# Attention in steps of 128 queries instead of 64, the first two blocks in alternating halves, and a new order

## The chip, the cores and the metric

The kernel runs on one core of a Trainium2 chip. TensorE (PE) multiplies matrices into PSUM, VectorE (DVE), ScalarE (ACT) and GpSimd (POOL) work element by element, and SyncE (SP) issues the loads and stores, which 16 DMA engines carry. Everything is one launch. The metric is the time of one execution in microseconds; lower is better. The time before is 1117.62 us, the median of three runs (1113.61 to 1118.52).

## What is computed

Local attention with eight memory keys feeds a rational feed-forward layer, and that feeds a gated one:

```python
# q, k, v: 4 batches x 8 heads x 768 x 64; for each chunk of 32 queries
k_full = concat([mem_k, k[c_start-16 : c_end+8]])          # 64 keys
a = softmax(q_c @ k_full.T / 8);  attn = a @ v_full
x  = attn as 3072 tokens x 512
h  = x @ w_in                                              # 512 -> 2048
P  = a[0] + a[1]*h + a[2]*h**2 + a[3]*h**3
Q  = 1 + |b[0]|*|h| + |b[1]|*h**2
x2 = (P / (Q + 1e-6)) @ w_out                              # 2048 -> 512
out = ((x2 @ w1) * (x2 @ w2)) @ w3 @ w_out2                # 512 -> 1024 -> 1024 -> 512
```

## The kernel before

**Blocks and units.** The 3072 tokens are eight blocks of 384. The first layer (`ffn1`) goes through 128 *units*, 16 for each block; unit n takes one slice of 128 of the 2048 hidden columns. A unit is twelve matmuls into a PSUM tile `h` (`gemm1`), a chain of elementwise steps on ACT, DVE and POOL (the functions `rat_...`, `g_hi`, `g_lo`; the four tiles are `W`, `Q`, `A` and `h`), and twelve matmuls that add to four PSUM banks `acc` (`gemm2`). Each product is three matmuls, since every operand is kept as a high part and a low part. `SEQ` lists the units. Before the change block 0 does its first eight slices, then block 1 all sixteen, then block 0 its other eight; at each such change of block the four `acc` banks are put away (`spill`), and block 0's first half is read back (`half_back`) and added (`half_add`).

**Weights.** They come as 64-bit numbers, 512 KB for each slice of 128. `decode` turns a slice into its high and low part: ACT and DVE shift and join the bits (`scale`, `low`, `join`), ACT writes the high part, DVE or POOL the low part. The 16 slices of `w_in` go to `wA`, those of `w_out` to `wB`, and all 32 are decoded while the first two blocks run. `MODES` says for each slice which engines and which PSUM ring (`h` or `att`) it uses.

**Attention.** A step `u` takes 64 queries of all heads: loads (`load_qk`, `load_v`), scores on PE (`s_pe`), maximum, difference, exponential, sum, inverse and product (`s_max` to `s_norm`), transposes (`t_pe`), a copy by ACT and one by DVE into `aT` (`t_copy`), the product with v (`v_pe`), and the split of the result into the two parts of `xr`, which is the block's x (`v_parts`). Six steps make a block. `qk`, `v` and `e` have two buffers each. Chunk 0's keys stand together in the loaded tile; chunk 1's are the memory keys and the last 56, which DVE or POOL copy into a second tile `k` (`second_keys`, L291). The norm runs on POOL (L343). From block 1 on, the outputs of a step and the scores of the next are one piece of PE work in one PSUM bank (`vs_pe`), and the ring `att`, from which these pieces and the transposes take their bank, has one bank.

**After the first layer** the program makes the gate's products for blocks 0 and 1 (`ab`), the product of w3 and the last weights (`w3o`), and then blocks 2 to 7 in pairs (`pr`) with the last product (again `acc`, 512 wide).

**Order.** `order()` is a planner that runs when the program is built. Every piece of work is a `step` with a due time, an assumed cost for each engine that can do it, what it comes after, and what buffers it takes and frees. Due times are in units and come from tables (`R`, `DI`, `SI`, `TG`, `XT` and others). It decides the order in which instructions stand on each engine, and the engine itself where there is a choice; on the chip each engine then takes its instructions in that order and waits for what each one needs.

## Time and profile before

| what | value |
|---|---|
| median of three runs | 1117.62 us (1113.61 to 1118.52) |
| the profiled execution, and its span | 1116.94 us, 1115.2 us |
| PE, DVE, ACT, POOL busy | 1061.4, 763.4, 700.4, 511.3 us |
| data moved, mean rate | 104.03 MB, 93 GB/s |

The span runs from the first to the last instruction of the profiled execution; 1.74 us lie around it. Matmuls follow one another in a pipeline, so a PE that is busy all the time still goes faster or slower with what stands in its queue; its time is read from the starts of its matmuls. The stretches in the rows below are cut at events of this program: the first matmul into `h` (46.24 us), the first `h` of unit 8 (105.76), the end of the `h` of unit 39 (256.6), a point in the units of block 7 (612), the end of the `h` of the last unit (675.5), a point just after the first `w3o` (745), and one after the last `w3o` and the waits behind it (840).

### The profile page before, as it was taken

What the parts mean: (1) busy time and instruction counts of PE and PEld (TensorE: products, weight loads), DVE (VectorE), ACT (ScalarE), POOL (GpSimd) and SP (SyncE); (2) the same over time, 40 slices, a digit from 0 to 9 for tenths busy, and PEclk for the clock granted to TensorE, in tenths of its full rate; (3) what the DMA queues carried; (4) which work ended last, traced back from release to release, by engine and by line L of the source; (5) the groups of instructions that cost most, each with busy time, mean ns of one, the idle gap of its engine ahead of it and who ended that gap; (6) DMA issues with size and microseconds to landing.
All of it is one profiled execution on the core that took longest, in us unless ns stands there. A gap on an engine that the chain in (4) does not pass through costs nothing.

```text
span 1115.2 us, 20447 instructions
## 1 busy us (share of the span) xinstructions
PE 1061.4 (95%) x7632; PEld 989.4 (89%) x7632; DVE 763.4 (68%) x1495; ACT 700.4 (63%) x1363; POOL 511.3 (46%) x513
## 2 busy tenths in 40 slices
PE   5587899999999999999999998999999999999998
PEld 3486888989999999999999998998779999998997
DVE  5888989778687777677777887776564662563330
ACT  3686998768687787777877997744343252343322
POOL 1454665445454454444444566642223343335233
PEclk9998999999999999999999999999999999999999
DMA  8835331322121121111220324643433321312201
GB/s 220 231 96 171 115 109 52 110 71 63 44 71 43 52 82 44 56 57 44 79 84 35 114 76 133 208 134 131 134 131 114 114 85 50 112 39 78 74 20 57
DMA packets 42468, 104.03 MB, mean 93 GB/s; under 512 B 6208, under 2 KB 6336, under 8 KB 42368
## 3 DMA queue, kind: packets, MB, share of 16 engines
q1 hardware_dynamic: 42080, 102.65, 29.2%
q8 instruction: 60, 0.98, 0.4%
q14 instruction: 40, 0.33, 0.1%
q10 hardware_dynamic: 288, 0.07, 0.0%
HBM read 85.14 MB, written 17.56 MB: 92 GB/s over the span
## 4 chain that ended last, share of the span: by engine, by line
PE 72%; DVE 12%; ACT 8%; DMA 5%; issue 2%; SPq 1%; POOL 0%; DVEq 0%; POOLq 0%; ACTq 0%
PE acc L275 27%; PE h L275 18%; PE pr L275 14%; PE ab L275 5%; PE w3o L275 3%; DMA qk<-in_qkT_dram 3%; PE at L365 2%; PE at L312 2%; DVE w L248 2%; ACT A L399 1%; DVE A L416 1%; ACT Q L407 1%; ACT W L399 1%; DMA sr<-sd 1%; ACT Q L423 1%
## 5 line engine op out<-in xcount | busy, mean ns | idle before, releaser
L275 PE MATMUL h<-xr,wA 128*128 128x384 f32 x1536 | 296.4, 342 | 11.6 <-DVE A L437 8.6
L275 PE MATMUL acc<-gh,wB 128*128 128x384 f32 x1024 | 287.0, 343 | 1.5 <-POOL wB L259 1.2
L275 PEld LDWEIGHTS h<-xr,wA 128*128 128x128 f32 x1536 | 270.3, 190 | 16.8 <-DVE A L437 10.8
L411 POOL TENSOR_TENSOR W<-W,Q 128x384 f32<-128x384 f32 x128 | 130.8, 1022 | 168.3 <-ACT Q L407 116.9
L275 PEld LDWEIGHTS acc<-gh,wB 128*128 128x128 f32 x1024 | 188.0, 190 | 5.6 <-POOL wB L259 1.9
L275 PE MATMUL acc<-gl,wB 128*128 128x384 f32 x512 | 173.4, 339 | 1.9 <-POOL gl L446 1.9
L446 POOL TENSOR_TENSOR gl<-A,gh 128x384 fp32r<-128x384 f32 x128 | 132.0, 1032 | 51.2 <-ACT gh L441 41.4
L275 PE MATMUL pr<-wB,wA 128*128 128x384 f32 x624 | 114.4, 335 | 1.0 <-ACT W L932 0.9
L429 DVE SCALAR_TENSOR_TENSOR A<-A,cf,h 128x384 f32<-128x384 f32 x128 | 77.9, 608 | 51.6 <-ACT h L425 51.1
L275 PEld LDWEIGHTS pr<-wB,wA 128*128 128x128 f32 x624 | 108.9, 188 | 3.2 <-ACT W L932 1.2
L275 PEld LDWEIGHTS acc<-gl,wB 128*128 128x128 f32 x512 | 97.1, 190 | 3.3 <-POOL gl L446 3.3
L399 ACT ACTIVATE A<-h,cf 128x384 f32<-128x384 f32 x128 | 85.1, 665 | 22.7 <-PE h L275 21.9
L423 ACT ACTIVATE Q<-W,one 128x384 f32<-128x384 f32 x128 | 78.6, 614 | 28.4 <-POOL W L411 28.1
L407 ACT ACTIVATE Q<-W,cf 128x384 f32<-128x384 f32 x128 | 90.7, 709 | 3.8
L275 PE MATMUL acc<-wB,gh 128*128 128x512 f32 x294 | 92.2, 394 | 0.0
L416 DVE TENSOR_TENSOR A<-A,h 128x384 f32<-128x384 f32 x128 | 70.2, 548 | 30.1 <-ACT W L399 16.8
L441 ACT CAST gh<-A 128x384 fp32r<-128x384 f32 x128 | 64.8, 506 | 39.3 <-DVE A L437 39.0
L939 POOL TENSOR_TENSOR A<-A,Q 128x384 f32<-128x384 f32 x24 | 24.5, 1020 | 124.1 <-DVE A L939 124.1
L418 DVE SCALAR_TENSOR_TENSOR A<-A,cf,h 128x384 f32<-128x384 f32 x128 | 77.9, 609 | 2.9 <-ACT W L399 0.8
L433 DVE SCALAR_TENSOR_TENSOR h<-W,one,h 128x384 f32<-128x384 f32 x128 | 78.5, 614 | 0.1
L939 DVE TENSOR_TENSOR A<-pr,W 128x384 f32<-128x384 f32 x48 | 26.7, 556 | 69.5 <-PE pr L275 68.9
L437 DVE SCALAR_TENSOR_TENSOR A<-h,A 128x384 f32<-128x384 f32 x128 | 70.4, 550 | 1.3
(123 smaller groups left out, 1846.3 us busy)
## 6 DMA issues: line engine op xcount, KB each, us to landing
qk<-in_qkT_dram SPq DMA_DIRECT2D x96, 160.0 KB
w<-in_w_out_dram SPq DMA_DIRECT2D x24, 512.0 KB
sr<-sd SPq DMA_DIRECT2D x48, 256.0 KB
w<-in_w_in_dram SPq DMA_DIRECT2D x16, 512.0 KB
w<-in_w3T_dram SPq DMA_DIRECT2D x16, 512.0 KB
w<-in_w_dram SPq DMA_DIRECT2D x16, 512.0 KB
v<-in_vW_dram SPq DMA_DIRECT2D x48, 128.0 KB
out_dram<-oo SPq DMA_DIRECT2D x24, 256.0 KB
```

What stands on the lines that cost most here:

```text
L275: pe.matmul(out_, lhsT=wi(w, a), rhs=xi(x, c), start=first and i == 0, stop=last and i == 2, skip_group_check=more)
L399: act.activation(out=t, in_=hps[n][src], func=func, scale=scale, bias=bias)
L407: act.activation(out=t, in_=hps[n]["W"], func=AF.Identity, scale=cf[:, 5:6], bias=cf[:, 4:5])
L411: pool.tensor_tensor(out=W, in0=W, in1=Q, op=ALU.mult)
L416: dve.tensor_tensor(out=A, in0=A, in1=h, op=ALU.mult)
L418: dve.scalar_tensor_tensor(out=A, in0=A, scalar=cf[:, 1:2], in1=h, op0=ALU.add, op1=ALU.mult)
L423: act.activation(out=Q, in_=W, func=AF.Ln, bias=one)
L429: dve.scalar_tensor_tensor(out=A, in0=A, scalar=cf[:, 0:1], in1=r, op0=ALU.add, op1=ALU.mult)
L433: dve.scalar_tensor_tensor(out=r, in0=W, scalar=one, in1=r, op0=ALU.add, op1=ALU.mult)
L437: dve.scalar_tensor_tensor(out=A, in0=r, scalar=-2.0, in1=A, op0=ALU.add, op1=ALU.mult)
L441: act.copy(out=gh, in_=hps[n]["A"])
L446: eng.tensor_tensor(out=gl, in0=hps.pop(n)["A"], in1=gt[n].bitcast(F32), op=ALU.subtract)
```

## The change

Attention goes in steps of 128 queries (two windows of 64 side by side, `NS` = 2). `qk`, `v` and `e` have one buffer each instead of two. A copy of the memory keys is kept behind each window in the tile, loaded once a batch, so both chunks find their 64 keys in a row and the copies into `k` are gone. The norm may go to POOL or DVE; the planner puts all 24 on DVE. Scores and outputs are separate pieces of PE work. Blocks 0 and 1 alternate in halves: eight units of block 0, eight of block 1, then the second halves, so both put a half away and add it later. The constant 1 + 1e-6 of the rational function is an immediate instead of a tile `one`. The planner's costs, due times, `MODES` and the leads of attention are new. The matmuls are the same in number and shape.

```diff
+NS = 2
+UQ = NS * QB
+UPS = S // UQ
+NU = B * UPS
-UPB = N // QB
+UPB = N // UQ
-HF = NF1 // 2
-SEG = [(0, 0, HF), (1, 0, NF1), (0, HF, NF1)] + [(b, 0, NF1) for b in range(2, NB)]
+HF = 8
+SEG = [(0, 0, HF), (1, 0, HF), (0, HF, NF1), (1, HF, NF1)] + [(b, 0, NF1) for b in range(2, NB)]
...
-    q_t = atp.tile([P, 2, HG, QB + KW], F32, name="qk")
-    k_t = [atp.tile([P, HG, CK], F32, name=f"k{i}") for i in range(2)]
-    v_t = [atp.tile([P, H, D], F32, name=f"v{i}") for i in range(2)]
-    e_t = [atp.tile([P, 2 * NCH, CK], F32, name=f"e{i}") for i in range(2)]
+    q_t = [atp.tile([P, HG, NS, QB + KW + NMEM], F32, name=f"qk{i}") for i in range(QBUF)]   # QBUF = 1
+    v_t = [atp.tile([P, NS, H, D], F32, name=f"v{i}") for i in range(VBUF)]                  # VBUF = 1
+    e_t = [atp.tile([P, NG, CK], F32, name=f"e{i}") for i in range(EBUF)]                    # EBUF = 1
...
     def load_qk(u):
+        b, j = divmod(u, UPS)
+        t = q_t[u % QBUF]
         for g in range(2):
-            sp.dma_start(out=q_t[g * D:(g + 1) * D, u % 2], in_=qkT[b, j, :, g * HG:(g + 1) * HG])
-    def second_keys(u, mem, eng):
-        k = slice(0, NMEM) if mem else slice(W1, KW)
-        eng.tensor_copy(out=k_t[u % 2][:, :, :NMEM] if mem else k_t[u % 2][:, :, NMEM:],
-                         in_=q_t[:, u % 2, :, QB + k.start:QB + k.stop])
+            r, h = slice(g * D, (g + 1) * D), slice(g * HG, (g + 1) * HG)
+            for s in range(NS):
+                sp.dma_start(out=t[r, :, s, :QB + KW], in_=qkT[b, j * NS + s, :, h])
+            if j < QBUF:
+                for s in range(NS):
+                    sp.dma_start(out=t[r, :, s, QB + KW:], in_=qkT[b, 0, :, h, QB:QB + NMEM])
...
-    def s_norm(u):
-        e = e_t[u % 2]
-        pool.tensor_tensor(out=e, in0=e, in1=sums.pop(u).to_broadcast([P, 2 * NCH, CK]), op=ALU.mult)
+    def s_norm(u, eng):
+        e = e_t[u % EBUF]
+        eng.tensor_tensor(out=e, in0=e, in1=sums.pop(u).to_broadcast([P, NG, CK]), op=ALU.mult)
...
-    def vs_pe(u, tag, outputs, scores):
-        b = bank(tag, "at")
-        if outputs:
-            v_pe(u, b[:, :KC * QB])
-        if scores:
-            s_pe(u + 1, b[:, KC * QB:])
...
-            act.activation(out=Q, in_=W, func=AF.Ln, bias=one)
+            act.activation(out=Q, in_=W, func=AF.Ln, bias=ONE)
-        dve.scalar_tensor_tensor(out=r, in0=W, scalar=one, in1=r, op0=ALU.add, op1=ALU.mult)
+        dve.scalar_tensor_tensor(out=r, in0=W, scalar=ONE, in1=r, op0=ALU.add, op1=ALU.mult)
...
-    MODES = "KnNhaMNhhNNNNNNhmMNmHNhHaAHMamNn"
+    MODES = "KNnhahkKkNNNNNNNHNmmHAaMAaaaANAn"
-    TG, TO, TM = 0.82, 1.09, 0.41
+    TG, TO, TM = 1.727, 0.363, -0.182
```

The first place is VectorE's queue from its first instruction on. Before, `k` is the second key tile, `mx`, `sm` and `r` are the maximum, sum and inverse, `w` and `wx` are weights being decoded.

```order
L291 COPY k_85<-qk 128x4x56
L291 COPY k_86<-qk 128x4x56
L320 MEMSET sc 128x2x16
L322 TENSOR_REDUCE mx<-sc 128x4
L325 TENSOR_TENSOR e_89<-sc,mx 128x256
L333 TENSOR_REDUCE sm<-e_89 128x4
L337 TENSOR_SCALAR r<-sm 128x4
L338 RECIPROCAL r<-r 128x4
L322 TENSOR_REDUCE mx<-sc 128x4
L325 TENSOR_TENSOR e_90<-sc,mx 128x256
L291 COPY k_85<-qk 128x4x56
L246 SCALAR_TENSOR_TENSOR wx<-wx,w_133 128x512
```

On VectorE the same place, the first step of attention, now reads as follows.

```order
L334 MEMSET sc 128x2x16
L336 TENSOR_REDUCE mx<-sc 128x8
L339 TENSOR_TENSOR e_85<-sc,mx 128x512
L347 TENSOR_REDUCE sm<-e_85 128x8
L255 SCALAR_TENSOR_TENSOR wx<-wx,w_145 128x512
L351 TENSOR_SCALAR r<-sm 128x8
L352 RECIPROCAL r<-r 128x8
L257 SCALAR_TENSOR_TENSOR wx<-w_145,wx 128x512
L357 TENSOR_TENSOR e_85<-e_85,r 128x512
L255 SCALAR_TENSOR_TENSOR w_147<-w_147 128x512
L268 TENSOR_TENSOR wA<-wx,wA 128x512
```

The copies are gone, one instruction of 512 takes the place of two of 256, and the norm (`e<-e,r`) now stands in VectorE's queue, behind a join of the weights.

The second place is SyncE's queue from the first load on. Before, `qk` is queries and keys, `v` the values, `w` a slice of weights.

```order
L287 DMA qk<-in_qkT_dram 64x640 x2
L296 DMA v_87<-in_vW_dram 64x512
L298 DMA v_87<-in_vW_dram 8x512
L299 DMA v_87<-in_vW_dram 56x512
L287 DMA qk<-in_qkT_dram 64x640 x2
L296 DMA v_88<-in_vW_dram 64x512
L298 DMA v_88<-in_vW_dram 8x512
L299 DMA v_88<-in_vW_dram 56x512
L228 DMA w_133<-in_w_in_dram 128x1024
L287 DMA qk<-in_qkT_dram 64x640 x2
```

On SyncE the opening now reads as follows, from the second instruction on (one load of `qk` in two stands ahead of it).

```order
L302 DMA qk_83<-in_qkT_dram 64x4x8 x2
L299 DMA qk_83<-in_qkT_dram 64x4x160 x2
L302 DMA qk_83<-in_qkT_dram 64x4x8 x2
L308 DMA v_84<-in_vW_dram 64x512
L309 DMA v_84<-in_vW_dram 56x512
L311 DMA v_84<-in_vW_dram 8x512
L308 DMA v_84<-in_vW_dram 64x512
L309 DMA v_84<-in_vW_dram 56x512
L311 DMA v_84<-in_vW_dram 8x512
L237 DMA w_145<-in_w_in_dram 128x1024
L237 DMA w_147<-in_w_in_dram 128x1024
L299 DMA qk_83<-in_qkT_dram 64x4x160 x4
```

The second step's loads used to stand ahead of the first weights, as it had a buffer of its own; now four of them come behind two slices of weights, and they wait until the scores of the first step have read the only buffer. Each load of `qk` that was 64 runs of 640 numbers is 64 x 4 runs of 160, and the first step brings 64 x 4 x 4 runs of 8 for the memory keys.

The third place is TensorE's queue at the `w3o` part.

```order
L275 MATMUL acc<-wB 128x512 x9
L275 MATMUL w3o<-wB,w_9076 128x512 x12
L275 MATMUL w3o<-wB,w_9096 128x512 x12
L275 MATMUL ab<-xr,wA 128x384 x12
L275 MATMUL w3o<-wB,w_9149 128x512 x12
L275 MATMUL w3o<-wB,w_9154 128x512 x12
L275 MATMUL acc<-wB 128x512 x9
L275 MATMUL ab<-xr,wA 128x384 x12
L275 MATMUL w3o<-wB,w_9226 128x512 x12
L275 MATMUL w3o<-wB,w_9242 128x512 x12
L275 MATMUL acc<-wB 128x512 x9
L275 MATMUL w3o<-wB,w_9306 128x512 x12
```

On TensorE the same place now reads as follows.

```order
L284 MATMUL acc<-wB 128x512 x9
L284 MATMUL w3o<-wB,w_8579 128x512 x12
L284 MATMUL w3o<-wB,w_8599 128x512 x12
L284 MATMUL ab<-xr,wA 128x384 x12
L284 MATMUL w3o<-wB,w_8658 128x512 x12
L284 MATMUL w3o<-wB,w_8666 128x512 x12
L284 MATMUL acc<-wB 128x512 x9
L284 MATMUL ab<-xr,wA 128x384 x12
L284 MATMUL w3o<-wB,w_8725 128x512 x12
L284 MATMUL w3o<-wB,w_8741 128x512 x12
L284 MATMUL acc<-wB 128x512 x9
L284 MATMUL ab<-xr,wA 128x384 x12
```

A pair of `w3o` rows is one product. Before, `acc` followed it at once and the next product followed that; now a product of the gate (`ab`, 12 matmuls) is put in after an `acc` one time more in this excerpt, and in the whole part five times instead of three.

## Rows read from the trace of the kernel before

**Rows 1.** Stretches: length; busy PE, PEld, DVE, ACT, POOL; granted clock; DMA share, GB/s

```profile
0.00:46.24 46.24, 21.24 (x334) 14.52 (x334) 30.58 (x80) 20.35 (x44) 12.94 (x21) 1.00 0.84 225
46.24:105.76 59.52, 50.27 (x458) 44.83 (x458) 51.76 (x104) 47.05 (x94) 32.72 (x34) 0.91 0.45 137
105.76:256.60 150.84, 141.61 (x1140) 134.51 (x1141) 129.55 (x263) 125.80 (x250) 82.07 (x82) 0.99 0.31 98
256.60:612.00 355.40, 355.21 (x3149) 341.92 (x3148) 266.05 (x581) 272.61 (x545) 170.54 (x194) 1.00 0.18 57
612.00:675.50 63.50, 61.16 (x347) 59.99 (x347) 54.83 (x94) 59.74 (x115) 40.37 (x37) 1.00 0.30 100
...
745.00:840.00 95.00, 92.72 (x416) 76.44 (x415) 57.12 (x108) 38.91 (x64) 21.85 (x16) 1.00 0.45 149
840.00:1115.20 275.20, 271.31 (x1410) 250.46 (x1409) 118.82 (x184) 89.81 (x169) 106.47 (x96) 1.00 0.22 71
```

**Rows 2.** The timeline of the opening, TensorE (start, length)

```profile
3.96 0.42 PE L312 MATMUL sc<-qk 64*32 64x64 f32 x2 [3.96 <-DMA qk<-in_qkT_dram]
...
46.24 4.24 PE L275 MATMUL h<-xr,wA 128*128 128x384 f32 x12 [0.23 <-ACT xr L382]
```

**Rows 3.** The chain of waits, its longest pieces in the opening (start, us)

```profile
7.38 5.45 DMA qk<-in_qkT_dram
...
14.57 6.48 DMA qk<-in_qkT_dram
```

**Rows 4.** The DMA queues: packets, MB, share of 16 engines

```profile
q1 hardware_dynamic: 42080, 102.65, 29.2%
...
q10 hardware_dynamic: 288, 0.07, 0.0%
```

**Rows 5.** VectorE, groups by shape (count, busy us, mean ns, idle before)

```profile
L333 DVE TENSOR_REDUCE sm<-e 128x4 f32<-128x256 f32 x48 | 19.8, 412 | 2.7 <-ACT e L329 2.4
...
L518 DVE TENSOR_TENSOR wB<-w3o,wB 128x512 fp32r<-128x512 f32 x7 | 4.8, 692 | 20.7 <-ACT wB L516 20.7
...
L291 DVE COPY k<-qk 128x224 f32<-128x224 f32 x29 | 11.7, 403 | 17.5 <-DMA qk<-in_qkT_dram 17.4
...
L337 DVE TENSOR_SCALAR r<-sm 128x4 f32<-128x4 f32 x48 | 15.3, 318 | 0.3
...
L433 DVE SCALAR_TENSOR_TENSOR h<-W,one,h 128x384 f32<-128x384 f32 x128 | 78.5, 614 | 0.1
...
L437 DVE SCALAR_TENSOR_TENSOR A<-h,A 128x384 f32<-128x384 f32 x128 | 70.4, 550 | 1.3
```

**Rows 6.** ScalarE, groups by shape

```profile
L423 ACT ACTIVATE Q<-W,one 128x384 f32<-128x384 f32 x128 | 78.6, 614 | 28.4 <-POOL W L411 28.1
...
L425 ACT ACTIVATE h<-Q 128x384 f32<-128x384 f32 x128 | 63.0, 492 | 3.1 <-DVE sm L333 0.3
```

**Rows 7.** TensorE in the steady part, timeline (start us, length us)

```profile
335.35 0.34 PE L275 MATMUL acc<-gh,wB 128*128 128x384 f32 x1
...
335.62 0.69 PE L365 MATMUL at<-aT,v 128*64 128x64 f32 x16
...
336.23 0.43 PE L312 MATMUL at<-qk 64*32 64x64 f32 x16
...
336.81 2.37 PE L275 MATMUL h<-xr,wA 128*128 128x384 f32 x12
...
339.02 0.33 PE L275 MATMUL acc<-gh,wB 128*128 128x384 f32 x1
...
351.10 2.27 PE L275 MATMUL h<-xr,wA 128*128 128x384 f32 x12
...
353.20 0.33 PE L275 MATMUL acc<-gh,wB 128*128 128x384 f32 x1
```

**Rows 8.** TensorE where the first layer ends and among w3o, timeline

```profile
673.31 2.35 PE L275 MATMUL h<-xr,wA 128*128 128x384 f32 x12 [1.31 <-DVE A L437]
...
793.14 0.50 PE L275 MATMUL acc<-wB 128*128 128x512 f32 x1 [0.46 <-ACT wB L516]
```

More of the change, by code (lines that the diff above doesn't have):

```diff
@@ L259, in low_part @@
             eng.tensor_tensor(out=d[0][:, 1], in0=value(), in1=d[0][:, 0].bitcast(F32), op=ALU.subtract)
-        a = step(t, {"dma": 1.9}, load, *early, take=("raw",))
+        a = step(t, {"dma": 2.0}, load, *early, take=("raw",))
         s = step(t, {"act": 0.58}, scale, a, take=(tag,) if tag else ())
-        c = step(t, {"act": 0.58} if byte else {"dve": 0.335}, low, a, port=not byte)
-        J = {"dve": 0.66}
+        c = step(t, {"act": 0.58} if byte else {"dve": 0.38}, low, a, port=not byte)
+        J = {"dve": 0.64 if tag else 0.72}
         c = step(t, J, lambda: join(0), s, c, port=not tag)
@@ new lines, in attend @@
+        outs(u, t + 1.3 * k, k)
+    R = (-1.427,0.216,0.543,0.964,1.286,6.975,-0.116,0.555,0.902,0.154,1.541,1.594,-0.009,-1.683)
+    DI = -2.973
+    DO = -3.438
+    WI, WO = {}, {}
+    SI = 0.893
+    SO = 0.844
+    DJ = -3.554
+    DP = -3.457
+    SJ = 0.944
+    chunks = sorted([(SI * f + DI if f < HF else SJ * (USE[f] - USE[HF]) + DJ + USE[HF], 0, f) for f in range(NF1)]
+                    + [(SO * f + LAG + 0.45 + DO if f < HF else SJ * (USE[f] - USE[HF]) + LAG + 0.45 + DP + USE[HF], 1, f) for f in range(NF1)])
@@ L714, in attention_rational_mlp_gated_mlp @@
     for n in range(n1):
-        while u <= NU and max(0, int(pos(u)) - (LEAD if u >= 3 * UPB else 4)) < n:
+        while u < NU and lead(u) < n:
             attend(u)
@@ L1101, in attention_rational_mlp_gated_mlp @@
             now += AFT
+    for x, n in late:
+        x.after.append(G1[n])
     done = order()
```

252 lines of the change are left out of this document (118 added, 134 removed).

## Prediction

> **What bounds the kernel now.** I read the busy times first (table above): TensorE works 1061.4 of 1115.2 us, so 53.8 us of waits are left. The stretches show where they lie [rows 1]; the first column is the length, the second TensorE's busy time: 25.0 us before the first matmul into h (46.24 less 21.24), 9.3 until block 1 is attended (105.76), 9.2 until 256.6, 0.2 in the whole steady part from 256.6 to 612, then 2.3, 2.3 and 3.9 in the last three rows shown. In the steady part the time is the sum of the PE pieces, and no other engine can change it. In the second stretch VectorE is busy 51.76 of 59.52 us, 87%, and TensorE waits for weights and scores that VectorE has yet to make; there the time goes with VectorE's work. The first stretch is bound by something else: VectorE is at 66%, the DMA engines at 0.84, the first scores start only when the loads are there [rows 2], and the chain of waits has pieces of 5 and 6 us that are loads of qk [rows 3]. TensorE also runs slowly there: twelve matmuls take 4.24 us at 46.24 [rows 2] and 2.27 in the steady part [rows 7], that is at the lower level of its clock, 1.2 instead of 2.4 GHz; the granted clock of the second stretch, 0.91, holds what is left of this.
>
> **The prices on VectorE.** An instruction on 256 columns takes 0.412 us, one on 512 takes 0.692 [rows 5], so one in place of two saves 0.13, and the five of a step of 128 (maximum, difference, sum, copy into aT, low part) save 0.66. The inverse is on a few columns, so one falls away at its full 0.318 [rows 5]. A copy into k costs 0.403 [rows 5] and goes. The norm comes to VectorE: 512 columns, 0.692. GpSimd loses it, which pays nothing by itself, since GpSimd is at 55% in the second stretch [rows 1].
>
> **The opening, up to 46.24 us.** Block 0 is three steps: 3 x (0.66 + 0.318 - 0.692) is 0.9, and 8 copies that stand ahead of its last split make 3.2, in all 4.1 us less. As VectorE is not what binds here, I take half, 2.0 us. The loads can undo it. The first scores must now wait for twice the queries; a step's load of qk was 256 runs of 2560 bytes and is 1024 of 640. Queue q1 spent 0.292 x 16 x 1115.2, or 5210 us of engine time, on 42080 packets, 124 ns for one of 2.44 KB on average; q10 spent under 9 us (a share below 0.05%) on 288 of about 240 bytes, under 31 ns each [rows 4]. So on 16 engines a step's qk takes between 2.0 us (64 x 31 ns) and 7.9 us (64 x 124), against 2.1 before, and in the first step the memory keys, 1024 runs of 32 bytes, add up to 2.0. With one buffer, three such loads stand one behind another, each behind the scores before. I take 3.3 us (31 ns, and 400 further bytes at q1's 19.7 GB/s, 51 ns for one run), as 640 bytes are nearer to the small packets: 1.2 us a step, which the half credit above leaves room for. Bounds for the stretch: 6 us earlier to 15 us later.
>
> The Trainium skill speaks against this edit: "Perfetto Trace Analysis", Contiguity and DMAs, says that contiguity matters within a partition's line, and here 640 numbers in a row there become four pieces. It also has a threshold, "DMA: Bandwidth & Descriptors", Specifications: from 512 B a transfer can reach line rate. By that the 640-byte runs would cost what they did, and the opening's sum would be 2.0 us earlier without the 1.2 a step; no row here shows a run of 640 bytes.
>
> **From the first h to the end of block 1.** Three steps again save 0.9; 3 copies 1.2; three joins of the decoding fewer stand ahead of block 1's last split in the new order (34, not 37), at about 0.69 each, 2.1, which come back later; eight units of the immediate in place of the tile one at 0.064 (0.614 against 0.550 [rows 5]), 0.5. Together 4.7, over the 87% that VectorE is busy: 5.3 us. Against it: in the new order TensorE has six second products behind it when unit 8 begins, not eight. The two are 24 matmuls of 0.175 us (2.10 us for twelve, from 351.10 to 353.20 [rows 7]), 4.2 us that are still to be done. Part of them fits into the 9.2 us of waits of the third stretch; I take 2.0 (bounds 0 and 4.2). Opening and this stretch together: -2.0 - 5.3 + 4.2 - 2.0, or -5.1 us.
>
> **The pieces of attention on TensorE.** In the steady part a piece of outputs and scores lies between an acc at 335.35 and the next acc behind the following h at 339.02: 3.67 us, of which thirteen matmuls are 2.28. It costs 1.39 us: 0.61 outputs, 0.58 scores, 0.20 at its ends [rows 7]. Two of them make 2.78. A step of 128 does 1.22 and 1.16 with 0.20 or 0.40 at the ends, as outputs and scores now stand apart: 2.58 to 2.78. Over the 21 steps from block 1 on this is 0 to -4.2 us; I take -1.0, as pieces that stand apart come close to the upper figure. If each has to wait for its data besides, this term turns; that is a rival below.
>
> **The halves of block 1.** Four more adds at some 0.55 (the price of L437 [rows 5]) and four more transfers. The banks must be free before the next half's second products; the order fills the gap with two or three h in a row. With that cover gone, it is 2.2 us. I take +0.5.
>
> **The end of the first layer, 612 to 675.5.** ScalarE is busy 59.74 of 63.50 us while it decodes the gate's weights, and TensorE waits 2.3 us in this stretch [rows 1], the longest time 1.31 for A [rows 8]. The logarithm with its tile for the 1 takes 0.614, the exponential without one 0.492 [rows 6]; with an immediate it saves between 0 and 0.12 in each of 16 units, up to 2.0 us of ScalarE's time, and VectorE has 1.0 less. The new order also puts products of the gate between the last second products. I take -2.0 (bounds 0 and -4).
>
> **The w3o part.** TensorE waits 2.3 us in it [rows 1]; the wait at 793.14 is an acc directly behind its w3o, 0.46 us for ScalarE's copy of the result [rows 8]. The order now has five products of the gate among them, not three. I take -1.0 (bounds 0 and -2); the rest of the program keeps its instructions.
>
> **The sum.** -5.1 - 1.0 + 0.5 - 2.0 - 1.0 is -8.6 us. The profiled execution took 1116.94 us (its span and 1.74 around it), 0.7 below the median. That gives 1108.3; I say **1108**.
>
> **Rivals.**
> *The loads hold the opening.* If a run of 640 bytes costs 95 ns, between the bounds, a load of qk takes 6.1 us, 4.0 more than before, three times, and 2.0 for the memory keys: up to 14 us, of which the chain can hide what lies behind the softmax of the step before. For it speak the qk pieces in the chain [rows 3] and the single buffer; against it that the parts of a step are fewer. With 8 of the 14 showing, 1116. The Trainium skill, "Perfetto Trace Analysis", Contiguity and DMAs, points this way.
>
> *The opening gains in full.* If the softmax chain binds it and not the loads, half as many chains of a little greater length bring the first h to some 8 us earlier than my sum has it, and the waits of the third stretch halve (4.6): about 1096.
>
> *Slower: the one bank.* From block 1 on, scores, transposes and outputs all need the one bank of att, and TensorE takes its queue in order. If VectorE's norm stands behind other work, TensorE stands at the transposes or the outputs with all its matmuls queued behind. The place is the steady part, which has no waits now to absorb it. From 0.4 us in each of 21 steps the gain is gone; at 1 us it is 1129. Against it: by the new order four pieces of 2.1 us stand between scores and transposes, and the chain is about 3.5 us of VectorE (five times 0.692), one instruction of ScalarE, and hand-overs.
>
> *The change doesn't do what it says.* If the logarithm's immediate saves nothing, the end of the first layer gives 0 to -1 instead of -2; this moves the sum by a microsecond or two, not the verdict.
>
> **How the numbers follow.** Forecast (1100 to 1112, its own range) 0.48; opening in full 0.16; loads 0.22; one bank 0.14. What a measurement of this kernel tells from no change is some 0.5%, 5.6 us: faster is below 1112, slower above 1123. The forecast and the full opening are faster, 0.64; the loads are about the same, with a little of the bank, 0.23; the rest of the bank is slower, 0.13. The range is 1095 to 1120: it takes in the loads and most of the full opening, and leaves out under 2 in 10.
>
> **What would show it.** The first h of 12 matmuls between 40 and 48 us; no wait of the scores for qk above 5 us after the first; unit 8's first h near 98 us with two second products outstanding; VectorE's share in the second stretch still near 87%; the steady part with under 1 us of waits, and outputs and scores of a step costing 2.6 to 2.8 us; L433's successor at 0.55 us, the logarithm at 0.50 to 0.61. I am wrong if the first h comes after 52 us, if the steady part shows waits at the transposes or outputs, or if the two second products fall into no wait.

## Result and the profile after

The kernel after takes 1083.45 us (median of four runs, 1081.48 to 1086.56) against 1118.07 for the kernel before beside it: a ratio of 0.970, with a 95% interval of 0.966 to 0.974. The forecast was 1108, its range 1095 to 1120: the direction was right, and the gain is 34.6 us where 8.6 were summed up. The profiled execution has a span of 1082.5 us. Its page gives the busy times and the queue of the loads:

```profile
PE 1040.6 (96%) x7632; PEld 985.5 (91%) x7632; DVE 759.1 (70%) x1326; ACT 671.6 (62%) x1290; POOL 483.9 (45%) x438
...
q1 hardware_dynamic: 65440, 104.36, 31.5%
```

TensorE's busy time fell from 1061.4 to 1040.6 us and what is left of the span from 53.8 to 41.9, so about two thirds of the gain is work that became shorter and one third waits that went. The stretches of the kernel after, cut at the same events as [rows 1] (first h, first h of unit 8, end of the h of unit 39, the same unit of block 7, end of the last h, just after the first `w3o`, behind the last):

```profile
0.00:44.28 44.28, 17.17 (x364) 14.07 (x365) 26.45 (x50) 18.60 (x33) 7.67 (x10) 0.77 0.91 232
44.28:94.61 50.33, 40.72 (x408) 37.67 (x405) 46.78 (x83) 42.61 (x83) 24.96 (x21) 0.91 0.55 155
94.61:241.90 147.29, 145.76 (x1233) 140.51 (x1234) 134.93 (x247) 124.48 (x246) 82.70 (x77) 0.98 0.39 118
241.90:589.40 347.50, 347.50 (x3078) 338.48 (x3077) 263.11 (x487) 260.07 (x509) 154.52 (x152) 1.00 0.22 63
589.40:647.75 58.35, 58.35 (x338) 58.35 (x338) 54.26 (x97) 57.58 (x114) 41.03 (x36) 1.00 0.31 103
704.50:801.00 96.50, 96.50 (x456) 83.28 (x455) 62.23 (x110) 38.70 (x65) 25.32 (x18) 1.00 0.43 142
801.00:1082.50 281.50, 277.82 (x1443) 256.98 (x1441) 125.97 (x194) 91.97 (x172) 109.35 (x96) 1.00 0.22 73
```

Length less TensorE's busy time is the wait. Up to the first h it is 27.1 us (25.0 before), in the second stretch 9.6 (9.3), in the third 1.5 (9.2), then 0, 0 and 0 (0.2, 2.3 and 2.3), and 3.7 at the end (3.9). The third stretch is where the most waits went. Since the two orders do not hold the same products at the same event, the gain is also shown against the work done: all 5232 matmuls of 384 and 512 columns in each trace are counted in the order of their starts, at 0.1745 and 0.2333 us, and the table gives the time at which each kernel had done so much of this work.

| us of such matmuls done | before | after | gain so far |
|---|---|---|---|
| 0 (first h) | 46.2 | 44.3 | 2.0 |
| 40 (h of unit 11) | 116.4 | 108.2 | 8.2 |
| 180 (h of unit 44 done) | 283.1 | 267.6 | 15.5 |
| 460 (h of unit 111 done) | 604.0 | 582.5 | 21.6 |
| 560 (the gate's products) | 710.0 | 681.9 | 28.1 |
| 700 (`w3o` done) | 853.2 | 821.5 | 31.7 |
| end of the span | 1115.2 | 1082.5 | 32.7 |

From 180 to 460 both kernels do the same wide matmuls and neither waits; the 6.2 us gained there (321.0 against 314.8) are shorter pieces of attention, as a later section shows. The first row is no sure gain: kernels that differ in nothing ahead of the first h reach it at 43.0 to 46.2 us in the old order, and at 42.8 to 44.7 in the new one.

VectorE's and ScalarE's groups by shape (count, busy us, mean ns, idle before) answer to [rows 5, 6]:

```profile
L439 DVE SCALAR_TENSOR_TENSOR h<-W,h 128x384 f32<-128x384 f32 x128 | 70.8, 553 | 0.0
L357 DVE TENSOR_TENSOR e<-e,r 128x512 f32<-128x512 f32 x24 | 18.8, 784 | 0.1
...
L347 DVE TENSOR_REDUCE sm<-e 128x8 f32<-128x512 f32 x24 | 16.3, 679 | 7.0 <-ACT e L343 7.0
...
L429 ACT ACTIVATE Q<-W 128x384 f32<-128x384 f32 x128 | 66.9, 523 | 18.2 <-POOL W L417 18.1
```

The immediates do what they say: VectorE's product went from 0.614 to 0.553 us, the logarithm from 0.614 to 0.523. One instruction of 512 columns takes 0.68 us, as the prediction took it; the norm takes 0.784, not 0.692.

### The profile page after: what moved, and what is told of

Read it like the earlier page. It is cut to its first block, busy times and chain, and to the rows that moved or that the text cites. A ratio compares the mean times of both kernels' runs of the same rounds, so it can differ in the third digit from the quotient of the medians.

```text
span 1082.5 us, 20045 instructions
## 1 busy us (share of the span) xinstructions
PE 1040.6 (96%) x7632; PEld 985.5 (91%) x7632; DVE 759.1 (70%) x1326; ACT 671.6 (62%) x1290; POOL 483.9 (45%) x438
## 4 chain that ended last, share of the span: by engine, by line
PE 84%; DVE 6%; ACT 6%; DMA 2%; SPq 1%; issue 1%; DVEq 0%; ACTq 0%
PE acc L284 32%; PE h L284 21%; PE pr L284 16%; PE ab L284 6%; PE w3o L284 4%; PE sc L326 2%; PE xo L380 2%; PE at L362 1%; DMA w<-in_w_out_dram 1%; DMA w<-in_w_in_dram 1%; DVE A L435 1%; ACT Q L413 1%; DVE h L439 1%; DVE A L443 1%; DVE A L422 1%
## 5 line engine op out<-in xcount | busy, mean ns | idle before, releaser
L284 PE MATMUL acc<-gh,wB 128*128 128x384 f32 x1024 | 282.9, 339 | 0.0
L417 POOL TENSOR_TENSOR W<-W,Q 128x384 f32<-128x384 f32 x128 | 133.6, 1044 | 210.8 <-ACT Q L413 192.2
L452 POOL TENSOR_TENSOR gl<-A,gh 128x384 fp32r<-128x384 f32 x128 | 135.2, 1056 | 74.8 <-ACT gh L447 69.7
L422 DVE TENSOR_TENSOR A<-A,h 128x384 f32<-128x384 f32 x128 | 70.4, 550 | 50.1 <-ACT A L405 49.6
L435 DVE SCALAR_TENSOR_TENSOR A<-A,cf,h 128x384 f32<-128x384 f32 x128 | 78.0, 609 | 33.2 <-ACT h L431 32.1
L405 ACT ACTIVATE W<-h 128x384 f32<-128x384 f32 x128 | 62.5, 489 | 49.2 <-PE h L284 47.2
L931 POOL TENSOR_TENSOR A<-A,Q 128x384 f32<-128x384 f32 x24 | 26.7, 1114 | 120.2 <-DVE A L931 117.1
L424 DVE SCALAR_TENSOR_TENSOR A<-A,cf,h 128x384 f32<-128x384 f32 x128 | 78.2, 611 | 3.2
L431 ACT ACTIVATE h<-Q 128x384 f32<-128x384 f32 x128 | 63.3, 495 | 24.5 <-DVE A L424 21.4
L429 ACT ACTIVATE Q<-W 128x384 f32<-128x384 f32 x128 | 66.9, 523 | 18.2 <-POOL W L417 18.1
L443 DVE SCALAR_TENSOR_TENSOR A<-h,A 128x384 f32<-128x384 f32 x128 | 70.9, 554 | 2.8
```

Of the source, the lines that this page charges most:

```text
L284: pe.matmul(out_, lhsT=wi(w, a), rhs=xi(x, c), start=first and i == 0, stop=last and i == 2, skip_group_check=more)
L405: act.activation(out=t, in_=hps[n][src], func=func, scale=scale, bias=bias)
L417: pool.tensor_tensor(out=W, in0=W, in1=Q, op=ALU.mult)
L422: dve.tensor_tensor(out=A, in0=A, in1=h, op=ALU.mult)
L424: dve.scalar_tensor_tensor(out=A, in0=A, scalar=cf[:, 1:2], in1=h, op0=ALU.add, op1=ALU.mult)
L429: act.activation(out=Q, in_=W, func=AF.Ln, bias=ONE)
```

## The experiments

Every kernel was timed beside the kernel before. In the sets that follow, that one stood at 1116.2 to 1117.1 us; the kernel after stood at 1083.45 and, timed again, at 1084.02. Differences to the kernel after are differences of medians, against 1083.45 unless another is named. "The count" is that of the work done, as in the table above. The theories A, B and C are those of the expectation printed with each run.

### The immediates, taken out of after and put into before

In the kernel after:

```diff
-            act.activation(out=Q, in_=W, func=AF.Ln, bias=ONE)
+            act.activation(out=Q, in_=W, func=AF.Ln, bias=one)
...
-        dve.scalar_tensor_tensor(out=r, in0=W, scalar=ONE, in1=r, op0=ALU.add, op1=ALU.mult)
+        dve.scalar_tensor_tensor(out=r, in0=W, scalar=one, in1=r, op0=ALU.add, op1=ALU.mult)
```

and the reverse in the kernel before.

> The kernel after the change with the tile one back in place of the immediate, in the logarithm on ScalarE and in the product on VectorE that takes the 1; the order of all instructions is that of the kernel after, so that only durations change. The logarithm should go from 0.523 us to about 0.61 and VectorE's product from 0.55 to about 0.61. Theory A (the prediction's: the immediates pay only where ScalarE or VectorE bind, that is in the units of the first two blocks and in the last block of the first layer): 1.5 to 3 us slower than the kernel after, 1085 to 1086.5. Rival B (the waits that went from the end of the first layer, 4.2 us there, went because of the immediates): 5 us or more slower, above 1088. Rival C (they do nothing): within 0.7 us of the kernel after.

> The kernel before with the two immediates and nothing else, in its own order. Theory A: 1 to 3 us faster than the kernel before, 1115 to 1117. Rival B (the immediates remove the waits at the end of the first layer): 4 us faster or more, 1114 or less, with TensorE's waits between 612 and 690 us down from about 5 to about 1. Rival C: no change, 1118.

Out of the kernel after: 1085.77 (1084.89 to 1086.15), 2.3 slower, with an interval (0.972 to 0.976) that overlaps that of the kernel after. Into the kernel before: 1111.95, ratio 0.996 (0.994 to 0.998), 5.2 faster. The groups of the kernel after with its tile again show the old prices:

```profile
L430 ACT ACTIVATE Q<-W,one 128x384 f32<-128x384 f32 x128 | 78.6, 614 | 16.8 <-POOL W L418 16.2
...
L440 DVE SCALAR_TENSOR_TENSOR h<-W,one,h 128x384 f32<-128x384 f32 x128 | 78.6, 614 | 0.0
```

Theory A fits the first run. In the old order the same edit is worth 5.2 us, as much as B said, but not where B said: of TensorE's waits between 605 and 690 us 3.3 of 4.0 are left, and by the count 3.7 us are gained by the time of unit 40, 1.0 where the layer ends and 1.1 behind it. Of the 3.7 us, 3.2 are there at the first h (43.0 us), ahead of any use of an immediate, so one profile does not settle where the gain lies. By the medians the edit is worth twice as much in the old order; the lower end of its interval there is 2.3 us, the figure of the new order, so the doubling is not shown.

### The tables of the second half, exchanged

In the kernel after (and the reverse in before):

```diff
-    TG, TO, TM = 1.727, 0.363, -0.182
+    TG, TO, TM = 0.82, 1.09, 0.41
-    PB = 0.164
+    PB = 1.23
-    DW, D3, DV = -6.212, -1.893, -1.702
+    DW, D3, DV = -7.706, -8.758, -0.644
-    LG2 = 3
+    LG2 = 2
-    XT, XS, SL, SH, GT, OT = -6.742, -5.180, -1.545, 0.934, -2.825, -0.532
+    XT, XS, SL, SH, GT, OT = -24.0, -16.0, 1.5, 0.6, 2.0, 0.0
```

> The kernel after the change with the due times of the second half as they were before (TG, TO, TM, PB, DW, D3, DV, LG2, XT to OT), the first half as it is. Theory A (the new order of the second half brings the 3.3 us of the w3o part, the 2 to 2.7 us behind it, and part of the 4.2 us of waits at the end of the first layer): 5 to 9 us slower than the kernel after, 1088 to 1092. Rival B (these stages gained because of what comes ahead of them, and the due times matter little): within 2 us of the kernel after.

> The kernel before with the due times of the second half of the kernel after, and nothing else. Theory A: 5 to 9 us faster than the kernel before, 1109 to 1113, with the w3o part some 3 us shorter. Rival B: within 2 us of the kernel before, or slower, since the due times were chosen for another first half.

The kernel after with the old tables: 1091.77 (1090.17 to 1091.90), 8.3 slower. By the count it loses 5.5 us where the first layer ends, 2.2 in the `w3o` part and 0.8 behind it. TensorE's waits there, of the kernel with the old tables, 615 to 700 us (what, total us, times, longest):

```profile
PE ab L284 <- DVE A L443: 3.7, 1, 3.7
```

Just behind this wait, from 653.4 to 656.8 us, the granted clock is 0.50, the lower of the two levels (1.2 GHz); TensorE is busy all that time, which costs another 1.7 us, so wait and clock make 5.4 of the 5.5. In the kernel after no wait of TensorE is left between 600 and 700 us, and its clock stays at 1.00 there. Its timeline shows what stands in the gap, after the last unit's h (start, length):

```profile
645.48 2.25 PE L284 MATMUL h<-xr,wA 128*128 128x384 f32 x12
...
649.64 2.25 PE L284 MATMUL ab<-xr,wA 128*128 128x384 f32 x12
...
653.81 2.25 PE L284 MATMUL ab<-xr,wA 128*128 128x384 f32 x12
```

Products of the gate (`ab`) stand one by one between the last second products, each of which needs the elementwise chain of its unit; the chain's length is hidden. The kernel before with the new tables is slower, 1120.67 (ratio 1.004, 1.002 to 1.007): by the count it gains 3.7 us by the end of the layer and 3.9 from `w3o` on, and loses 8.9 among the gate's products in between, most of it in one wait (TensorE's timeline, the wait in brackets):

```profile
726.04 9.23 PE L275 MATMUL ab<-xr,wA 128*128 128x384 f32 x38 [5.84 <-DVE xr L490]
```

The gate's products wait there for VectorE's split of an x2 (L490), which stands behind six joins of the weights in VectorE's queue. So both sides are half right: the tables carry the gain of these stages, and only behind their own first half. A last run put the old due times of the second half's decoding back alone:

```diff
-    DW, D3, DV = -6.212, -1.893, -1.702
+    DW, D3, DV = -7.706, -8.758, -0.644
```

> The kernel after the change with the old due times of the second half's decoding alone (DW, D3, DV); the products' due times stay as after. Theory A (the earlier decoding of the gate's weights in the old table holds ScalarE and VectorE while the last units need them, and makes the 5.5 us at the end of the first layer): 4 us slower than the kernel after or more, above 1087.5. Rival B (the place of the gate's products among the last second products makes them): within 2 us of the kernel after.

1084.93 (1083.31 to 1086.67), 1.5 slower by the medians, with nearly the same interval (0.967 to 0.975). This fits rival B, but it does not single out the place of the products, which moved as well: the gate's products now stand in groups of 36 and 24 matmuls, a wait is back in front of the first group, and by the count 2.0 of the 5.5 us are lost (TensorE's timeline):

```profile
650.64 6.51 PE L284 MATMUL ab<-xr,wA 128*128 128x384 f32 x36 [1.78 <-DVE A L443]
```

### The tables of the first half

```diff
-    H0 = 1.272
+    H0 = 1.384
-    MODES = "KNnhahkKkNNNNNNNHNmmHAaMAaaaANAn"
+    MODES = "KnNhaMNhhNNNNNNhmMNmHNhHaAHMamNn"
-    R = (-1.427,0.216,0.543,0.964,1.286,6.975,-0.116,0.555,0.902,0.154,1.541,1.594,-0.009,-1.683)
+    R = (0.00,0.92,-0.04,0.23,0.42,0.36,0.33,0.22,0.91,0.83,1.16,1.53,1.21,2.10)
...
```

`a_tab1` has these and DI to SJ as before, `a_R` the R alone, `a_modes` the MODES alone.

> The kernel after the change with the planner's first-half tables as they were before: R (due times of the elementwise steps), H0, MODES (who decodes each slice of weights) and DI, DO, SI, SO, DJ, DP, SJ. Width, buffers, halves, immediates, attention's due times and the second half stay as after. Theory A (the order of the decoding and of the elementwise steps made most of the 10 us that came between unit 0 and unit 40): 6 us slower than the kernel after or more, above 1089, the loss ahead of unit 40. Rival B (the steps of 128, with fewer rounds of the chain, made them): under 3 us slower, below 1086.5.

> The kernel after the change with the old table R alone (due times of the elementwise steps of a unit). Theory A (R carries the first half's gain): 7 us slower than the kernel after or more, above 1090. Rival B (the plan of the decoding carries it): under 3 us slower, below 1086.5.

> The kernel after the change with the old MODES alone (which engines and which PSUM ring each slice of weights is decoded with). Theory A (R carries the first half's gain): under 3 us slower, below 1086.5. Rival B (the plan of the decoding carries it): 6 us slower or more, above 1089.5, with the loss between unit 12 and unit 25, where the kernel with all old first-half tables lost 10 us against the kernel after.

All together: 1094.50 (1093.12 to 1095.86), 11 slower. R alone: 1105.41 (1104.80 to 1105.93), 21.4 slower to the 1084.02 of its set. MODES alone: 1091.37 (1089.76 to 1093.23), 7.4 slower. So theory A holds in the first two runs and rival B in the third, and the tables are not shares of a sum: the old R alone costs twice what all the old tables cost together.

The reverse was run as well, the new R alone in the kernel before (`b_tabR`). Theory A there was that this order of the elementwise steps is better by itself, below 1113.5; rival B that it fits only the kernel that it was made for. It took 1121.19 (ten runs, 1118.05 to 1124.91, ratio 1.004, 1.002 to 1.005), 4.3 slower than the kernel before: rival B. In that order the program does not keep its result, so it stands for its time alone.

TensorE's waits from unit 8 on, of the kernel before (106 to 281 us), of the kernel with all old tables (100 to 272) and of the kernel with the old R alone (100 to 284):

```profile
PE h L275 <- DVE A L437: 4.7, 2, 2.8
...
PE h L284 <- DVE w L257: 5.7, 2, 3.5
...
PE h L284 <- DVE A L443: 8.6, 4, 2.9
PE at L362 <- DVE w L257: 2.5, 1, 2.5
```

and of the kernel after (94 to 266 us):

```profile
PE h L284 <- ACT xr L388: 2.3, 1, 2.3
...
PE h L284 <- DVE A L443: 0.4, 2, 0.2
```

Between 40 and 180 us of work done the old R costs 16.7 us, and two things make nearly all of it. TensorE's waits grow by 9.5 us. And four times its granted clock is at the lower level (0.50) for 3.4 us, from 108.7, 153.0, 176.9 and 187.2 us, each time within 1.5 us of the end of a wait of 2.1 to 3.0 us; half of the 13.3 us that it works in them, 6.7, is the price (an estimate). The kernel after has no such stretch there. In the rows of such stretches the granted clock is the number before the DMA's share (first the kernel with the old R, then the kernel after, over the same wide matmuls):

```profile
129.70:188.90 59.20, 48.92 (x394) 46.03 (x393) 51.34 (x92) 49.73 (x96) 32.23 (x30) 0.93 0.42 128
127.90:171.10 43.20, 42.62 (x329) 41.88 (x329) 40.85 (x76) 42.84 (x87) 31.38 (x28) 1.00 0.44 139
```

An h waits for a bank, which L443, the last step of an earlier unit's chain, gives back. VectorE's timeline shows the order of the last three steps (L435, L439, L443; L422 and L424 belong to the next unit). The kernel with the old R:

```profile
172.39 0.61 DVE L435 SCALAR_TENSOR_TENSOR A<-A,cf,h 128x384 f32<-128x384 f32 x1 [1.67 <-ACT h L431]
173.36 0.55 DVE L422 TENSOR_TENSOR A<-A,h 128x384 f32<-128x384 f32 x1 [0.36 <-ACT W L405]
173.83 0.56 DVE L439 SCALAR_TENSOR_TENSOR h<-W,h 128x384 f32<-128x384 f32 x1
174.29 0.61 DVE L424 SCALAR_TENSOR_TENSOR A<-A,cf,h 128x384 f32<-128x384 f32 x1
174.82 0.55 DVE L443 SCALAR_TENSOR_TENSOR A<-h,A 128x384 f32<-128x384 f32 x1
```

and the kernel after:

```profile
155.63 0.61 DVE L435 SCALAR_TENSOR_TENSOR A<-A,cf,h 128x384 f32<-128x384 f32 x1
156.16 0.56 DVE L439 SCALAR_TENSOR_TENSOR h<-W,h 128x384 f32<-128x384 f32 x1
156.75 0.56 DVE L443 SCALAR_TENSOR_TENSOR A<-h,A 128x384 f32<-128x384 f32 x1
157.22 0.55 DVE L422 TENSOR_TENSOR A<-A,h 128x384 f32<-128x384 f32 x1
```

From the start of L435 to the end of L443 it is 2.98 us in the first and 1.68 in the second, with the same instructions, and the next h of the first waits for that L443:

```profile
175.42 0.79 PE L284 MATMUL h<-xr,wA 128*128 128x384 f32 x3 [2.07 <-DVE A L443]
```

This shows how one wait arises; it does not show that the gain of R comes by it. The two places were picked, and over all units between 100 and 270 us the means lie close: 2.68 in the kernel before, 2.58 with the old R and 2.41 after. It is also short, 2.46, in the kernel before with the new R, which is slower. What makes R and the rest of the tables fit each other stays open. With the old MODES the loss is another: in the timeline of TensorE

```profile
150.04 0.44 PE L284 MATMUL acc<-gh,wB 128*128 128x384 f32 x1 [3.61 <-ACT x2o L469]
```

the second products wait for ScalarE to put a half away. In the kernel after ScalarE is busy 42.84 of the 43.20 us from 127.90 to 171.10 (in the row above), so it has no room for more of the decoding there.

### VectorE's work by itself

Added to the kernel after, in the six steps of the first two blocks (and left out of the kernel before, next):

```diff
+        for _ in range(2 if u < 2 * UPB else 0):
+            dve.tensor_copy(out=k_t, in_=k_t)
         mx = sums[u] = atp.tile([P, NG, 1], F32, tag="mx", bufs=2, name="mx")
```

> The kernel after the change with two idle copies of 128 x 224 on VectorE ahead of the maximum in each of the six steps of blocks 0 and 1, which stand for the copies of keys that went; the order is otherwise that of after, and only VectorE's time is added (12 x 0.40 = 4.8 us). Theory A (the prediction's: up to the end of block 1 the time goes with VectorE's work): 4 to 6 us slower, 1087.5 to 1089.5. Rival B (waits for loads and the order of the weights bind these stretches, VectorE has gaps): under 2 us slower, below 1085.5.

```diff
     def second_keys(u, mem, eng):
+        if u > 1:
+            return
...
     def s_inv(u):
+        if u % 2:
+            sums[u] = sums[u].rearrange("p (g o) -> p g o", o=1)
+            return
```

> The kernel before, in its own order, without the copies of the second keys from the third step on and without the inverse in every second step (those parts of the attention are left out of the computation). In the first two blocks VectorE has 9 copies of 0.40 us and 6 inverses of 0.32 us less, 5.5 us, about what the change takes from it there. Theory A (the prediction's: until block 1 is attended the time goes with VectorE's work): 4 to 7 us faster than the kernel before, 1110 to 1113, and the gain is there by unit 8 of block 1. Rival B (VectorE's time alone buys little; gaps take it up, as the added copies in the kernel after were taken up): under 2.5 us faster, above 1114.5.

In the profiles VectorE's busy time up to unit 8 is 4.1 us longer in the first and 4.0 shorter in the second. The first costs 1.2 us (1084.67, 1082.52 to 1085.44, inside the interval of the kernel after), the second gives 2.2 (1114.67, ratio 0.998, 0.996 to 0.999). Rival B in both. The waits of the outputs for `aT` grew from 8.2 in the kernel after to 10.1 us in the first of these two, and the wait for v behind them shrank from 5.5 to 3.8 (TensorE's waits, 0 to 100 us):

```profile
PE xo L383 <- DVE aT L376: 10.1, 3, 3.9
...
PE xo L383 <- DMA v<-in_vW_dram: 3.8, 1, 3.8
```

So this stretch pays some 0.3 to 0.55 us for each of VectorE's, and the first of these may be nothing; the prediction took 1.15.

### The norm on GpSimd

```diff
-    NORM = "pd"
+    NORM = "p"
```

> The kernel after the change with the norm on GpSimd in all 24 steps, as it was before (NORM = p; the planner places the rest again). Theory A (the norm's place matters: on GpSimd it stands behind other work, and before it TensorE waited 5.9 us for it at the transposes): 4 us slower than the kernel after or more, above 1087.5, with waits of the transposes for GpSimd in the first two blocks. Rival B (the price of 0.69 us on VectorE and the longer one on GpSimd about even out): within 2 us of the kernel after.

1086.13 (1083.61 to 1088.69), 2.7 slower, with an interval (0.969 to 0.974) that overlaps that of the kernel after. The planner placed other steps anew as well, so this stays undecided.

### The loads of the opening

```diff
-    QBUF, VBUF, EBUF = 1, 1, 1
+    QBUF, VBUF, EBUF = 1, 2, 1
```

> The kernel after the change with two buffers of v instead of one. In the kernel after, TensorE waits 5.49 us at 40.34 us for v, whose load may start only when the outputs of the step before are made. Theory A (the loads into single buffers hold the opening): the first h comes 4 us earlier or more and the end 3 to 5 us earlier, 1078 to 1080.5. Rival B (behind the first h the weights that VectorE and ScalarE decode set the pace): the first h comes earlier, the end within 1.5 us of the kernel after.

TensorE's timeline of the opening, its waits in brackets, of the kernel after:

```profile
17.56 1.11 PE L362 MATMUL at<-idn,e 128*128 128x128 f32 x4 [8.56 <-DVE e L357]
...
24.66 0.39 PE L326 MATMUL sc<-qk 64*32 64x64 f32 x2 [2.91 <-DMA qk<-in_qkT_dram]
...
40.34 2.10 PE L380 MATMUL xo<-aT,v 128*64 128x64 f32 x32 [5.49 <-DMA v<-in_vW_dram]
```

and with two buffers of v:

```profile
37.10 1.12 PE L362 MATMUL at<-idn,e 128*128 128x128 f32 x4 [4.36 <-DVE w L257]
39.70 1.97 PE L380 MATMUL xo<-aT,v 128*64 128x64 f32 x32 [1.47 <-DVE aT L373]
```

The wait for v is gone, and the last outputs start 0.6 us earlier: they now wait for the transposes, which wait behind a join of the weights. The first h comes at 43.5 against 44.3, within what two executions differ by, and the end is 4.6 us later (1088.02, 1087.57 to 1089.28). Theory A is refuted; rival B fits the opening, but not the end. The planner placed other steps anew from VectorE's fifth instruction on, so this is no test of the buffer alone.

### The halves

```diff
-SEG = [(0, 0, HF), (1, 0, HF), (0, HF, NF1), (1, HF, NF1)] + [(b, 0, NF1) for b in range(2, NB)]
+SEG = [(0, 0, HF), (1, 0, NF1), (0, HF, NF1)] + [(b, 0, NF1) for b in range(2, NB)]
+PRED = [0, 0, 1, 0] + list(range(2, NB - 2))
-FREE = [0, 0] + [LAST[b - 2] + 1 for b in range(2, NB)]
+FREE = [0, 0] + [LAST[PRED[b]] + 1 for b in range(2, NB)]
...
```

> The kernel after the change with the units in the old sequence: eight of block 0, all sixteen of block 1, the other eight of block 0, with the buffers of x and their order changed to fit (block 2 follows block 1's buffer). All else is as after. Theory A (the alternating halves cost about what the prediction took, 0.5 us, and give nothing else): within 2 us of the kernel after, 1081.5 to 1085.5, or faster by up to 2. Rival B (the halves let the attention of blocks 2 and 3 and the second half of the weights spread better, and the gain from unit 8 to 40 is theirs): 4 us slower or more, above 1087.5, with waits between 100 and 270 us.

> The kernel after the change with the old sequence of the halves, as in a_oldseg, in five rounds beside the kernel after itself. Theory A (the halves cost the 0.5 us that the prediction took, or up to 2): 0.5 to 2.5 us faster than a_same. Rival B (they make no difference and the first run fell low by chance): within 0.7 us of a_same.

> The kernel after the change, unchanged, as the measure for the other three runs: 1082 to 1085. Its first h may come within 2 us of the 44.28 us of the first profile, and what lies behind it is shifted by as much; a difference between two kernels in the opening that is not larger says nothing.

1081.56 (1080.83 to 1084.58), and in the longer set 1081.70 (1079.88 to 1082.78) beside 1084.02 (1081.89 to 1085.29) for the kernel after: 1.9 and 2.3 us faster, both times, with intervals that still touch (0.967 to 0.971 against 0.969 to 0.973). Theory A. This kernel, the change without its alternating halves, has the lowest median of all that were run.

### The width

```diff
-NS = 2
+NS = 1
...
-    QBUF, VBUF, EBUF = 1, 1, 1
+    QBUF, VBUF, EBUF = 2, 2, 2
...
-        sm = step(t + .55 * k, {"dve": 0.60}, lambda: s_sum(u), ex[u])
+        sm = step(t + .55 * k, {"dve": 0.37}, lambda: s_sum(u), ex[u])
```

(and the other costs of attention alike).

> The kernel after the change in steps of 64 queries (NS = 1), with two buffers of qk, v and e and the planner's attention costs halved or as they were before; the memory keys behind the window, the alternating halves, the immediates and all other tables stay as after. Theory A (the width pays: a step of 128 costs TensorE about 0.3 us less than two of 64, times 24, and VectorE 1.0 us less, which counts in the first two blocks): 8 to 16 us slower than the kernel after, 1091 to 1099; in the steady part the pieces of scores, transposes and outputs of 128 queries cost 3.2 us or more together against 2.95. Rival B (the width pays 1 us on TensorE, as the prediction took it, and the gain is the order's): 1 to 5 us slower, 1084 to 1088.5.

1149.69 (1146.80 to 1151.27): 66 us slower, far outside what either side said. Some 40 us are lost by the time at which 40 us of wide matmuls are done. Two of TensorE's waits there:

```profile
109.96 0.69 PE L362 MATMUL at<-idn,e 128*128 128x128 f32 x2 [4.00 <-POOL e L357]
...
129.86 0.66 PE L362 MATMUL at<-idn,e 128*128 128x128 f32 x2 [11.33 <-DVE w L257]
```

Six steps of block 1, each with three separate pieces in one bank, go round one after another, and units wait for the block's x. The kernel before had joined outputs and scores. The run thus does not price the width alone, and since buffers and planner costs changed with it, the cause of these 40 us is argued and not shown. What it does give is the price of a piece. In the steady part of the kernel after (TensorE's timeline):

```profile
238.23 0.34 PE L284 MATMUL acc<-gh,wB 128*128 128x384 f32 x1
238.50 1.15 PE L380 MATMUL xo<-aT,v 128*64 128x64 f32 x32
239.58 2.35 PE L284 MATMUL h<-xr,wA 128*128 128x384 f32 x12
...
243.68 0.34 PE L284 MATMUL acc<-gh,wB 128*128 128x384 f32 x1
243.95 1.10 PE L326 MATMUL sc<-qk 64*32 64x64 f32 x64
244.97 1.31 PE L284 MATMUL h<-xr,wA 128*128 128x384 f32 x6
```

From the last acc to the h, less the acc's own 0.17, outputs cost 1.18 us and scores 1.12. In the kernel with steps of 64:

```profile
386.68 0.33 PE L284 MATMUL acc<-gh,wB 128*128 128x384 f32 x1
386.94 0.65 PE L326 MATMUL sc<-qk 64*32 64x64 f32 x32
387.52 2.38 PE L284 MATMUL h<-xr,wA 128*128 128x384 f32 x12
```

scores cost 0.67, and outputs by the same reading 0.71 (mean of 22). Twice the work adds 0.45 to the scores and 0.47 to the outputs; 0.22 and 0.24 are fixed ends.

The steady part prices the whole step as well. From 180 to 460 us of work done every kernel of this record does the same 1605 wide matmuls, and TensorE has no wait in any of them. The five kernels with joined steps of 64 take 319.8 to 321.0 us for it, the thirteen profiles with steps of 128 take 314.8 to 315.5, whatever their tables, and this one, with separate steps of 64, takes 326.4. Less 280.1 for the wide matmuls (0.1745 each), 40.9 us are left for 25 steps of 64 in the kernel before and 34.7 for 12 steps of 128 in the kernel after: 3.27 and 2.89 us for 128 queries, 0.38 less.

## Why the prediction missed

**The failed step** is "Part of them fits into the 9.2 us of waits of the third stretch; I take 2.0 (bounds 0 and 4.2)". The two postponed second products are there (TensorE's busy time rose by 4.15, from 141.61 to 145.76), but the waits fell by 7.7 us, to 1.5. They had been priced as room for postponed work, with the new order of the steps left at no worth of its own. The runs show the order's worth: with the first half's old tables the kernel after is 11 us slower, and with the old R alone 21.4, of which 9.5 are waits that come back and 6.7 the lower clock behind them. At the start of unit 40 the sum had 5.1 us; it was 13.9 (258.88 to 244.97). Why this order and these tables fit each other is not shown: the new R in the kernel before made it slower.

**Up to the first h:** -2.0 forecast, -2.0 measured, VectorE's busy time 4.1 us less as worked out (30.58 to 26.45). That the time was met is luck: the kernel before with the immediates alone, whose opening is the same, had its first h at 43.0, 3.2 us earlier than the profile of the kernel before, so a difference of 2.0 between two profiles says nothing. The reason is not borne out either: the copies added back left the first h where it was (44.36 against 44.28), and taking the wait for v away moved it by 0.8.

**First h to unit 8:** -5.3 forecast, -9.2 measured, of which the two products postponed make 4.2. VectorE's work fell by 5.0 us (4.7 were summed), but the rule "there the time goes with VectorE's work" did not hold: TensorE's waits stayed (9.3 and 9.6), and VectorE's share rose to 93%. What became shorter is its busy time, by 9.5: 4.2 for those products, 2.6 for attention (10.94 to 8.34 in the groups of that stretch), the rest in the wide matmuls that stay, which took 0.216 us each before (41.40 for 192 records) and 0.197 after (33.31 for 169).

**The pieces:** -1.0 forecast with a bound of -4.2, the second term that was mis-sized. From the rows, 128 queries cost 2.87 us before (two of 1.29 and two transposes of 0.14) and 2.65 after (1.17, 1.12, 0.36), 0.22 less, or 4.5 in 21 steps. The steady part as a whole gives 0.38 a step, some 8 us in 21 (an estimate); what makes the difference between the two readings stays open. Wrong was the split of a piece [rows 7]: 0.61 and 0.58 were taken as work with 0.20 at the ends. Only 0.47 and 0.45 is work; a joined piece of 1.29 holds 0.37 of fixed ends.

**Halves:** +0.5 forecast, about +2 measured. **End of the first layer:** -2.0 (to -4); the waits there, 2.3 in that stretch and 1.4 behind it, are all gone, and by the count 6.5 us are gained. Of the two causes named, the new tables with the gate's products in the gaps carry it (5.5 us with the old tables); the immediate gave some 1.0 there in the old order and 0.3 in the new, where 1.5 of the 1.8 us that the tile costs in the profile are there by unit 40. **`w3o`:** -1.0; its 2.3 us of waits went, 3.6 by the count. Behind it 1.0 that the sum had at nothing.

**The rivals.** The loads did not hold the opening as that rival had it: the first h came no later, though TensorE's waits for loads ahead of it grew from 9.2 to 15.9 us (10.4 for qk and 5.5 for v). The trace keeps the time of every packet: a run of 640 bytes took 43 ns on average, where 51 was taken, and one of 32 bytes 9 ns, where 31 was taken; one of 2560 bytes took 143 before. So a step's qk is 2.75 us on 16 engines against 2.28, 0.5 more and not 1.2, and the memory keys are 0.6 us and not 2.0. The Trainium skill, "DMA: Bandwidth & Descriptors", Specifications, lets transfers of 512 B upward reach line rate. The trace agrees only in part: an engine moved 14.9 GB/s on the runs of 640 bytes, and 17.9 on those of 2560 before. The Trainium skill, "Perfetto Trace Analysis", Contiguity and DMAs, has contiguity matter within a partition's line. The trace agrees, with 172 ns for four pieces in place of 143 for one. The opening in full is not what happened either, since the first h stayed at 44.28. One bank: the steady part has no waits (347.50 of 347.50 us busy); the run with steps of 64 looks like this rival come true in block 1, which its mixed edit leaves unproven. That the immediates do nothing is refuted by their rows.

**What the runs add up to:** first-half tables 11, second-half tables 8.3, pieces 4.5 to 8, immediates 2.3, halves -2: 24 to 28 of 34.6 us. Each of these but the pieces is what the kernel after loses when one thing is taken back. They are not worth that by themselves: in the kernel before, the new second-half tables and the new R each made it slower (1120.67 and 1121.19). The rest lies in how these act on one another and stays open, and so does what the width does ahead of the steady part, as the one run on it changed more than the width.

## What to carry to other kernels

A new order is an edit with a price of its own, and waits in the old order are more than room for postponed work: a better order can remove them, and the lower clock behind them too. Its price belongs to the whole order; a table that is worth 21 us in one kernel made another slower. A stretch where an engine is busy 87% is not bound by it until adding work there has been seen to cost time; here 4.1 us added cost 1.2 at most. Before pricing a merged piece, take the fixed ends from two sizes of it, since one size cannot tell ends from work. A stretch without waits, cut at the same work in every kernel, prices a piece without any reading of single rows.

## What the hardware showed that was not expected

Two executions of one order can differ by 3 us in the opening: unit 8 starts at 94.6 us in the kernel after, at 94.2 in a second profile of it, and at 91.8 and 91.6 in the kernels with the old second-half tables or their decoding times, whose first half is the same; the distance to the first then stays, 2.6 and 3.0 us from unit 16 on, as far as the orders are one.

TensorE's granted clock is 0.77 in the first stretch after, where it waits 27 of 44 us. The 1.00 that [rows 1] gives for the opening before is no measurement: that trace has no clock record ahead of 50.2 us. Its matmuls show the lower level there, with 1.12 us for sixteen outputs at 42.91 and 0.69 at 50.41. So most of the opening ran at the lower level in both kernels, and the 0.91 of the second stretch before is not what is left of it, as the prediction read it, but two later stretches at 0.50, from 60.4 and from 94.5 us.

Short load packets were cheaper than the prediction took them: a run of 640 bytes cost a DMA engine 43 ns where 51 was taken, and one of 32 bytes 9 ns where 31 was taken from the small queue.
